# Last phase of a spectral-gate and squared-ReLU backward kernel: loads moved ahead, the gate multiply taken out of the weight-gradient copies, two terms moved to ScalarE

## The chip, the cores and the metric

The kernel runs on one core of a Trainium2 chip. The metric is the device time of one execution in microseconds: the median of nine runs before the change is 430.44 us (427.58 to 432.5). One execution was also taken by the hardware profiler; its span, from the first to the last instruction, is 428.8 us, and that execution's own time is 430.61 us.

A core has five engines that each run their own instruction list in order: TensorE (PE in the profile, its weight loads PEld) for matmuls, VectorE (DVE), ScalarE (ACT), GpSimd (POOL) and SyncE (SP), which here only issues DMAs. They wait for each other by semaphores. An engine that waits holds up all that stands behind in its own list.

## The reference, cut to what matters

The program computes a forward pass and all its gradients. `A_ref` is a 2-D real FFT of the normalized rows, multiplied by complex weights, and transformed back; `B_ref` is a two-layer MLP with squared ReLU; both stand behind a layer norm with a scale and a shift, and a gate, that come from a condition vector `c`.

```
mod = silu(c) @ w_mod                      # sa, ca, ga, sb, cb, gb
h = layernorm(x) * (1 + ca) + sa
x = x + ga * A_ref(h, A_w_r, A_w_i)        # irfft2(rfft2(h) * W)
h = layernorm(x) * (1 + cb) + sb
x = x + gb * B_ref(h, B_w1, B_b1, B_w2, B_b2)
return x
# reference(): the output, and the vector-Jacobian product with grad_out for
# A_x, A_w_r, A_w_i, B_w1, B_b1, B_w2, B_b2, c, w_mod
```

Sizes: 2048 rows of 512, a hidden size of 1792, all in bf16. The last phase of the kernel, which the change is about, produces three of the gradients. The gradient of `B_w2` is (squared ReLU of h) transposed times (gb * grad_out), 1792x512. That of `B_b2` is the column sum of gb * grad_out. That of `A_x` goes through the inverse transform of the spectral gradient and then the layer norm's backward formula, for each row: gx = v + n * a + b + gx1, where n is the normalized row, v the scaled gradient row, a and b two scalars of the row, and gx1 the gradient that came through the residual.

## The kernel before, in words

**Stages.** The forward spectral part and its back products run first (0 to about 100 us), then the MLP in four blocks of 512 rows, forward and backward (to about 283 us). Results that are needed later go to DRAM: the normalized rows (`n1_dram`), the squared ReLU (`h_dram`), the residual gradient (`gx1_dram`), the spectra. The rest is the end of the backward pass, in three stages:

1. *Spectral gradient* (`spec_f23` with `ew_b` and `after_b`, about 283 to 339 us). Eight groups `gi` of frequencies. Each group's weight gradients are made in a tile `gW` (three buffers in pool `ewb`, line 1166) and written by four DMAs (six for group 0) with rows of 257 elements (line 1170). Between the groups, `fill_w1` puts units of the `B_w1` gradient on TensorE (line 1126: 16 matmuls of 128x448 each), and `gms` emits columns of the `w_mod` gradient. `after_b` also issues the loads for what follows: the transform table `LG`, the first two tiles `hn` of the transposed squared ReLU (line 1067, DMA transposes), and all of grad_out as `g_sb` (line 1188, one DMA of 2 MB).
2. *`spec_g1`* (about 336.6 to 345.3 us). For each group TensorE makes two tiles `psG`; DVE copies one of them, ACT the other, into `CS` (lines 351 and 353).
3. *Row loop* (about 346 us to the end). Eight pairs of row tiles. For each pair: four small matmuls per tile into `psT` (line 375), a scaled copy `Tsb` on ACT (line 377), a matmul into `psY` (line 385), a copy `gs` on ACT, and then `row_pair`: on DVE the unfolding (lines 266 to 270), three products and row sums (lines 1278, 1281, 1285), the term gn = n * a + b (line 1289), and two sums (lines 1290, 1292); on ACT a scaled copy with a row sum (line 1280). The rows n1 and gx1 that it needs are loaded by `load_rows3` (lines 1222 and 1223). Between pairs, `fill` puts units on TensorE: first what is left of the `B_w1` gradient, then the 14 units `grad_w2` (line 1203: 16 matmuls of 128x512 into a PSUM buffer `mm`, of which there are two). DVE multiplies each `mm` by the gate row `modb[:, GB_B]` into `gw` (line 1206), and SyncE writes it out.

**What sets the order.** Engine lists are made by a scheduler that works through the program in the order written, by priorities (`high_priority`, `Priority`); `issue_after(x)` keeps an instruction behind x in the list. SyncE issues nearly all DMAs, in one list, on one hardware queue; eight counters are used in turn, so each DMA's issue waits until the one eight before it has landed. GpSimd issues a few writes on a queue of its own.

**Pools.** Tiles live in pools that are allocated and released like a stack at either end of the on-chip memory. When a pool is put where an earlier pool lay, the first instruction that writes a tile there waits for the last users of the old tiles in that place. In the kernel before, `gwp` (the tiles `gw`) is allocated behind `fin` (the loaded rows n1 and gxl), both after the spectral gradient, and `fin2` (the tiles `Tsb`, `gs`, `gn` and the rest of the row loop) follows at the same end when `spb` (the `Z` tiles) and `lg2` (the table `LG`) have been released.

Of the kernel before, what the change touches and what calls it, by code (L numbers as in the profile page):

```python
# [18 lines left out]
D = 512  # L19
# [316 lines left out]
def spec_g1(tc, K, Z, CS):  # L336
    nc = tc.nc
    with tc.tile_pool(name="psG", bufs=4, space=PSUM) as psG_pool, tc.tile_pool(name="psF", bufs=1, space=PSUM) as psF_pool:
        psF = psF_pool.tile([P, 4, P], FP32, name="psF")
        for gi in range(8):  # L340
            for hh in range(2):
# [8 lines left out]
                if hh == 0:  # L350
                    nc.vector.tensor_copy(out=dst, in_=src)
                else:
                    nc.scalar.copy(out=dst, in_=src)

            if gi % 2 == 1:
                for ri in range(2):
                    for n in range(2 * gi - 2, 2 * gi + 2):
                        q = 32 * (n % 4)
                        nc.tensor.matmul(psF[q:q + 1, n // 4, :], lhsT=Z[n // 2][:, n % 2, ri, 256:257], rhs=K["LG"][:, n, ri + 1, :],
                                         start=(ri == 0), stop=(ri == 1), tile_position=(0, q))  # L360
        for i in range(4):
# [82 lines left out]
class GMod:  # L444
# [13 lines left out]
    def emit(self, jc, q, row, pool, ppool):  # L458
# [8 lines left out]
        for dc in range(0, 4, 2):  # L467
            wmc = self.tiles[jc][dc // 2]
            gwm = pool.tile([P, 2, D], BF16, name="gwm", bufs=2)
# [11 lines left out]
def kernel(  # L481
# [580 lines left out]
    def load_hn():  # L1062
        fc = len(hns)
        if fc < NFC:
            pool = hnp if fc < 2 else endp.get("hn", endp["gw"])
            hns.append(pool.tile([P, NT, P], BF16, name="hn", bufs=2 if pool is not endp.get("hn") else 4))
            nc.sync.dma_start(hns[fc], h_dram[fc, :, :], transpose=True)

    lf2 = tc.alloc_tile_pool(name="lf2", bufs=1, side="right")
    gmp = tc.alloc_tile_pool(name="gmp", bufs=1, side="right")  # L1070
# [22 lines left out]
    def add_quadrants(ps, pool, out, scale=None):  # L1093
# [6 lines left out]
        def add():  # L1100
# [5 lines left out]
            if scale is not None:  # L1106
                nc.vector.tensor_tensor(row, row, scale, op=ALU.mult)
# [6 lines left out]
    def run_later(n=1):  # L1114
        if later:
            later[0][0] -= n
            if later[0][0] <= 0:
                later.pop(0)[1]()

# [29 lines left out]
    with tc.tile_pool(name="f23b", bufs=2) as fr, tc.tile_pool(name="ewb", bufs=2) as ew:  # L1149
# [22 lines left out]
        def after_b(gi):  # L1172
            if gi + 4 < 8:
                load(gi + 4)
            if gi == 3:
                with tc.issue_after(K["gW"]):
                    nc.sync.dma_start(K["LG"], LG_dram)
            fill_w1(2 if 0 < gi < 6 else 1)
            if gi == 4:
                with tc.issue_after(K["gW"]):  # L1180
                    load_hn()
                    load_hn()
            if gi == 5:
# [3 lines left out]
                with tc.issue_after(K["gW"]):  # L1187
                    K["g_load"] = nc.sync.dma_start(endp["g_sb"], g_view).ins
            if gi in (0, 1, 3, 4):
                gms.pop(0)[1]()  # L1190
                if len(gms) > 1:
                    gm.load(gms[1][0], gmp)
# [3 lines left out]
    fin = tc.alloc_tile_pool(name="fin", bufs=2, side="right")  # L1196
# [3 lines left out]
    def grad_w2(fc):  # L1200
        ps = mmps.tile([P, SB], FP32, name="mm")
# [3 lines left out]
        with tc.high_priority():  # L1205
            nc.vector.tensor_tensor(gw, ps, modb[:, GB_B, :], op=ALU.mult)  # L1206
        nc.sync.dma_start(out6_view[:, fc, :], gw)
        load_hn()

    def grad_b2():  # L1210
# [4 lines left out]
        add_quadrants(ps, gwp, out_7[None, :], modb[0:1, GB_B, :])  # L1215

    rows3 = {}

    def load_rows3(t):
        if t < NT:  # L1220
# [151 lines left out]
```

## Time and profile before

| | |
|---|---|
| median of nine runs | 430.44 us (427.58 to 432.5) |
| the profiled execution's time | 430.61 us |
| its span, first to last instruction | 428.8 us |
| busy over the span: PE / DVE / ACT / POOL | 396.3 / 354.5 / 256.2 / 55.1 us |
| clock granted to TensorE, mean | 0.994 of full |
| `spec_g1` on TensorE | 336.6 to 345.3 us |
| row loop, first `Tsb` to last `grad_w2` matmul | 348.6 to 423.6 us |

How to read it: a matmul is shown with the time from its start to its modelled end, and matmuls overlap, so that the distance between the starts of two matmuls is what one costs, and a busy PE is not yet a PE at its peak. DVE and ACT instructions overlap a little as well. Times after the first column are from the span's start. In a timeline, the bracket behind a row holds the idle time of that engine just before it and what ended the idle time. A DMA has two times: that of its issue on SyncE, and that of its landing.

### The profile page before, as it was taken

What the parts mean: (1) busy time and instruction counts of PE and PEld (TensorE: products, weight loads), DVE (VectorE), ACT (ScalarE), POOL (GpSimd) and SP (SyncE); (2) the same over time, 40 slices, a digit from 0 to 9 for tenths busy, and PEclk for the clock granted to TensorE, in tenths of its full rate; (3) what the DMA queues carried; (4) which work ended last, traced back from release to release, by engine and by line L of the source; (5) the groups of instructions that cost most, each with busy time, mean ns of one, the idle gap of its engine ahead of it and who ended that gap; (6) DMA issues with size and microseconds to landing.
All of it is one profiled execution on the core that took longest, in us unless ns stands there. A gap on an engine that the chain in (4) does not pass through costs nothing.

```text
span 428.8 us, 7116 instructions
## 1 busy us (share of the span) xinstructions
PE 396.3 (92%) x2353; PEld 195.3 (46%) x2375; DVE 354.5 (83%) x862; ACT 256.2 (60%) x487; POOL 55.1 (13%) x135
## 2 busy tenths in 40 slices
PE   2789999999899999999999999999999999897995
PEld 0344456654444444444444444455555654343332
DVE  6889868959996488968897998937997946998994
ACT  5578699678881187348635855464756464636331
POOL 7447930000000000000000000002221000000011
PEclk9999999999999999999999999999999999999899
DMA  8999899979496469778966998989999989999993
GB/s 240 222 264 299 238 241 314 294 247 203 159 357 219 122 115 336 186 159 199 299 170 179 172 311 261 298 177 313 281 275 294 175 237 189 223 276 265 261 248 116
DMA packets 144228, 101.11 MB, mean 236 GB/s; under 512 B 98970, under 2 KB 127519, under 8 KB 143807
## 3 DMA queue, kind: packets, MB, share of 16 engines
q1 hardware_dynamic: 141034, 93.03, 83.9%
q0 software_dynamic: 2592, 7.09, 5.4%
q10 hardware_dynamic: 564, 0.53, 0.4%
q8 instruction: 19, 0.31, 0.3%
q14 instruction: 19, 0.15, 0.1%
HBM read 35.44 MB, written 41.60 MB: 180 GB/s over the span
## 4 chain that ended last, share of the span: by engine, by line
PE 34%; DVE 25%; DMA 16%; ACT 14%; issue 5%; SPq 3%; POOL 2%; ACTq 0%; DVEq 0%
PE og L906 10%; PE mm L877 8%; DMA out_dram<-gW 6%; PE mm L712 5%; PE mm L1203 3%; DMA n<-n_dram 2%; DMA Xb<-xs_dram 2%; DVE jk L1285 2%; ACT gab L717 2%; PE psG L346 2%; DMA h_dram<-h 1%; DMA y<-gx_dram 1%; DMA wmc<-in_w_mod_dram 1%; ACT AE L329 1%; DMA out_dram<-x 1%
## 5 line engine op out<-in xcount | busy, mean ns | idle before, releaser
L712 PE MATMUL mm<-gT,w2T 128*128 128x512 bf16 x224 | 57.7, 383 | 3.1 <-ACT gab L717 3.1
L877 PE MATMUL mm<-h2T,w 128*128 128x512 bf16 x224 | 53.4, 378 | 1.6 <-ACT r L879 1.4
L1203 PE MATMUL mm<-g_sb,hn 128*128 128x512 bf16 x217 | 50.8, 382 | 2.3 <-DVE gw L1206 1.7
L906 PE MATMUL og<-w1T,gab 128*128 128x512 bf16 x218 | 49.9, 379 | 1.0 <-DVE o L971 0.8
L1126 PE MATMUL mm<-gab,h_sb 128*128 128x448 bf16 x256 | 50.7, 352 | 0.0
L906 PE MATMUL og<-w,h 128*128 128x512 bf16 x217 | 49.1, 379 | 0.3
L879 ACT ACTIVATE r<-mm,b1col 128x512 bf16<-128x512 f32 x56 | 37.0, 685 | 6.1 <-PE mm L877 3.3
L877 PEld LDWEIGHTS <-w 128*128 128x128 bf16 x224 | 21.1, 97 | 30.0 <-issue 8.3
L1203 PEld LDWEIGHTS <-hn 128*128 128x128 bf16 x224 | 21.4, 98 | 29.2 <-issue 5.8
L1126 PEld LDWEIGHTS <-h_sb 128*128 128x128 bf16 x256 | 24.6, 98 | 21.8 <-issue 0.6
L906 PEld LDWEIGHTS <-h 128*128 128x128 bf16 x224 | 21.8, 98 | 26.1 <-issue 0.9
L906 PEld LDWEIGHTS <-gab 128*128 128x128 bf16 x224 | 21.6, 98 | 25.9 <-issue 1.4
L712 PEld LDWEIGHTS <-w2T 128*128 128x128 bf16 x224 | 21.2, 98 | 22.6 <-issue 6.6
L1280 ACT ACTIVATE gs<-gn,inv 128x512 bf16<-128x512 bf16 x16 | 11.4, 715 | 24.8 <-DVE gn L1278 24.8
L919 ACT CAST G<-og 128x512 bf16<-128x512 f32 x16 | 9.2, 580 | 28.1 <-PE og L906 28.1
L295 POOL MEMSET AE<- 128x2 bf16 x4 | 0.3, 101 | 194.6 <-PE mm L877 194.6
L477 POOL DMA_DIRECT2D out_dram<-gwm x12 | 8.7, 730 | 118.4 <-DVE gx L1292 57.6
L881 DVE TENSOR_TENSOR h<-r 128x1024 bf16<-128x1024 bf16 x28 | 19.2, 687 | 4.8 <-ACT r L879 4.8
L717 ACT CAST gab<-mm 128x512 bf16<-128x512 f32 x36 | 21.3, 599 | 1.7 <-PE mm L712 1.5
L475 DVE SCALAR_TENSOR_TENSOR gm_junk<-wmc,onef,gmbc 128x512 bf16<-128x512 bf16 x24 | 18.0, 748 | 3.2 <-ACT gmbc L465 1.5
L715 DVE CAST gab<-mm 128x512 bf16<-128x512 f32 x20 | 13.8, 688 | 7.1 <-PE mm L712 6.8
L377 ACT ACTIVATE Tsb<-psT 128x512 bf16<-128x512 f32 x32 | 18.4, 607 | 1.5 <-PE psT L375 1.5
(290 smaller groups left out, 800.7 us busy)
## 6 DMA issues: line engine op xcount, KB each, us to landing
h_dram<-h SPq DMA_DIRECT2D x28, 256.0 KB, 3.3
gh_dram<-gab SPq DMA_DIRECT2D x28, 256.0 KB, 4.5
w<-in_B_w_dram SPq DMA_DIRECT2D x2, 1792.0 KB
wmc<-in_w_mod_dram SPq DMA_DIRECT2D x12, 256.0 KB, 5.3
out_dram<-gwm POOLq DMA_DIRECT2D x12, 256.0 KB, 6.4
wz_dram<-Z SPq DMA_DIRECT2D x8, 258.0 KB, 4.0
xs_dram<-Xs SPq DMA_DIRECT2D x8, 258.0 KB, 4.1
Z<-wz_dram SPq DMA_DIRECT2D x8, 258.0 KB, 5.7
```

What stands on the lines that cost most here:

```text
L377: nc.scalar.activation(Tsb, ps, AF.Copy, scale=EF_S)
L475: nc.vector.scalar_tensor_tensor(out=junk, in0=wmc[:, i, :], scalar=K["onef"], in1=gmbc, op0=ALU.mult, op1=ALU.mult, accum_out=self.gsc[:, ...
L712: nc.tensor.matmul(ps, lhsT=w2T[:, dc, fc * P:(fc + 1) * P], rhs=gT[b][:, :, dc, :], start=(dc == 0), stop=(dc == 3))
L715: nc.vector.tensor_copy(out=gaT[b][:, fc, :], in_=ps)
L717: nc.scalar.copy(out=gaT[b][:, fc, :], in_=ps)
L877: nc.tensor.matmul(ps, lhsT=w1[:, dc, (fc + i) * P:(fc + i + 1) * P], rhs=h2T[b][:, :, dc, :], start=(dc == 0), stop=(dc == 3))
L879: nc.scalar.activation(r[:, i, :], ps, AF.Relu, bias=b1col[:, fc + i:fc + i + 1])
L881: nc.vector.tensor_tensor(h2, r, r, op=ALU.mult)
L906: nc.tensor.matmul(ps, lhsT=lhs(fc), rhs=rhs[:, fc, :], start=(fc == 0), stop=(fc == NFC - 1))
L1126: nc.tensor.matmul(ps[:, 0:W4], lhsT=h2_sb[:, t, dc * P:(dc + 1) * P], rhs=ghn[t // 4][:, t % 4, fs], start=(t == 0), stop=(t == NT - 1))
L1203: nc.tensor.matmul(ps, lhsT=hns[fc][:, t, :], rhs=g_sb[:, t, :], start=(t == 0), stop=(t == NT - 1))
L1280: nc.scalar.activation(gs[:, i, :], gn[:, i, :], AF.Copy, scale=inv1[:, t + i:t + i + 1], accum_out=rr[:, i, 0:1])
```

## The change

- `grad_w2` no longer multiplies by the gate: its PSUM tile is copied to `gw` by ACT. Instead `g_sb` itself is multiplied by the gate row on DVE, in four pieces of 128x2048, one behind each of the last four groups of `spec_g1` (`scale_g`, called by the new argument `after`). `grad_b2`, which sums the same `g_sb`, loses its multiply at the end.
- The term gn = n * a + b of `row_pair` is made by ACT (an Identity activation with a scale and a bias per row) and no longer by DVE.
- Loads: those for the first two row pairs are issued behind `LG` in group 3 and no longer behind the last `gW` writes. `g_sb` is loaded in four DMAs of 0.5 MB behind the `gW` writes of group 4 and no longer behind those of group 5; the first two `hn` follow it and no longer go ahead of the writes of group 5. Row loads run three pairs ahead (`load_rows3(t + 6)`), the third of them in a tile of `fin2`. Each later `hn` is held behind a row load. The tiles `wmc` for the last two columns of the `w_mod` gradient are loaded together when t is 10.
- Pools: `fin` is allocated before the spectral gradient, so it no longer lies between the others; the order of releases follows. `gwm` gets four buffers at the end, and `b4` of `grad_b2` goes to another pool.

```diff
--- before.py
+++ after.py
@@ -333,7 +333,7 @@
         f3(7)
 
 
-def spec_g1(tc, K, Z, CS):
+def spec_g1(tc, K, Z, CS, after=None):
     nc = tc.nc
     with tc.tile_pool(name="psG", bufs=4, space=PSUM) as psG_pool, tc.tile_pool(name="psF", bufs=1, space=PSUM) as psF_pool:
         psF = psF_pool.tile([P, 4, P], FP32, name="psF")
@@ -348,7 +348,7 @@
                 dst = CS[:, :, :, n, :].rearrange("p t c b -> p c t b")
                 src = ps.rearrange("p h (y t b) -> p (h y) t b", y=2, b=8)
                 if hh == 0:
-                    nc.vector.tensor_copy(out=dst, in_=src)
+                    K["cast"] = nc.vector.tensor_copy(out=dst, in_=src).ins
                 else:
                     nc.scalar.copy(out=dst, in_=src)
 
@@ -358,6 +358,8 @@
                         q = 32 * (n % 4)
                         nc.tensor.matmul(psF[q:q + 1, n // 4, :], lhsT=Z[n // 2][:, n % 2, ri, 256:257], rhs=K["LG"][:, n, ri + 1, :],
                                          start=(ri == 0), stop=(ri == 1), tile_position=(0, q))
+            if after:
+                after(gi)
         for i in range(4):
             dst = CS[0:1, :, 1, i:16:4, :].rearrange("p t m b -> p m t b")
             src = psF[32 * i:32 * i + 1, :, :].rearrange("p m (t b) -> p m t b", b=8)
@@ -455,7 +457,7 @@
         for dc in range(0, 4, 2):
             self.tc.nc.sync.dma_start(self.tiles[jc][dc // 2], self.wm_view[:, dc:dc + 2, cs])
 
-    def emit(self, jc, q, row, pool, ppool):
+    def emit(self, jc, q, row, pool, ppool, nbuf=2):
 
         nc, K = self.tc.nc, self.K
         cs = slice(jc * D, (jc + 1) * D)
@@ -466,7 +468,7 @@
         junk = pool.tile([P, D], BF16, name="gm_junk", bufs=1)
         for dc in range(0, 4, 2):
             wmc = self.tiles[jc][dc // 2]
-            gwm = pool.tile([P, 2, D], BF16, name="gwm", bufs=2)
+            gwm = pool.tile([P, 2, D], BF16, name="gwm", bufs=nbuf)
             for i in range(2):
                 if i == 0:
                     nc.scalar.activation(gwm[:, i, :], gmbc, AF.Copy, scale=self.scf[:, dc + i:dc + i + 1])
@@ -1064,9 +1066,11 @@
         if fc < NFC:
             pool = hnp if fc < 2 else endp.get("hn", endp["gw"])
             hns.append(pool.tile([P, NT, P], BF16, name="hn", bufs=2 if pool is not endp.get("hn") else 4))
-            nc.sync.dma_start(hns[fc], h_dram[fc, :, :], transpose=True)
+            with tc.issue_after(K["rows" if fc < 4 else "rows0"]):
+                nc.sync.dma_start(hns[fc], h_dram[fc, :, :], transpose=True)
 
     lf2 = tc.alloc_tile_pool(name="lf2", bufs=1, side="right")
+    fin = tc.alloc_tile_pool(name="fin", bufs=2, side="right")
     gmp = tc.alloc_tile_pool(name="gmp", bufs=1, side="right")
     K["LF"] += [lf2.tile([P, 2, 3, P], BF16, name=f"LFb{gi}") for gi in range(4, 8)]
     W4 = 448
@@ -1090,7 +1094,7 @@
         nc.scalar.copy(out=b4, in_=ps[:, 0:W4])
         nc.gpsimd.dma_start(out_5.rearrange("(q f) -> q f", q=NFB), b4[0:P:32, :])
 
-    def add_quadrants(ps, pool, out, scale=None):
+    def add_quadrants(ps, pool, out):
         w = ps.shape[-1]
         b4 = pool.tile([P, w], BF16, name="b4", bufs=1)
         b4l = pool.tile([P, w], BF16, name="b4l", bufs=1)
@@ -1103,8 +1107,6 @@
                 nc.tensor.matmul(ps[0:1, 0:w], lhsT=K["ones_col"], rhs=x, start=(i == 0), stop=(i == 1))
             row = pool.tile([1, w], BF16, name="b4r", bufs=2)
             nc.scalar.copy(out=row, in_=ps[0:1, 0:w])
-            if scale is not None:
-                nc.vector.tensor_tensor(row, row, scale, op=ALU.mult)
             nc.sync.dma_start(out, row)
 
         later.append([4, add])
@@ -1116,6 +1118,16 @@
             later[0][0] -= n
             if later[0][0] <= 0:
                 later.pop(0)[1]()
+
+    rows3 = {}
+
+    def load_rows3(t):
+        if t < NT:
+            pool, n = (endp["fp"], 1) if t % 6 == 4 else (fin, 2)
+            rows3[t] = [pool.tile([P, 2, D], BF16, name=x, bufs=n) for x in ("n1", "gxl")]
+            nc.sync.dma_start(rows3[t][0], n1_dram[:, t:t + 2, :])
+            K["rows0"] = K.get("rows")
+            K["rows"] = nc.sync.dma_start(rows3[t][1], gx1_dram[:, t:t + 2, :]).ins
 
     w1o = {}
 
@@ -1175,64 +1187,63 @@
             if gi == 3:
                 with tc.issue_after(K["gW"]):
                     nc.sync.dma_start(K["LG"], LG_dram)
+                    load_rows3(0)
+                    load_rows3(2)
             fill_w1(2 if 0 < gi < 6 else 1)
+            if gi in (0, 1, 3, 4):
+                gms.pop(0)[1]()
+                if len(gms) > 1:
+                    gm.load(gms[1][0], gmp)
             if gi == 4:
-                with tc.issue_after(K["gW"]):
-                    load_hn()
-                    load_hn()
-            if gi == 5:
                 gmp.release()
                 endp["g"] = tc.alloc_tile_pool(name="gsp", bufs=1, side="right")
                 endp["g_sb"] = endp["g"].tile([P, NT, D], BF16, name="g_sb")
                 with tc.issue_after(K["gW"]):
-                    K["g_load"] = nc.sync.dma_start(endp["g_sb"], g_view).ins
-            if gi in (0, 1, 3, 4):
-                gms.pop(0)[1]()
-                if len(gms) > 1:
-                    gm.load(gms[1][0], gmp)
+                    for t in range(0, NT, 4):
+                        K["g_load"] = nc.sync.dma_start(endp["g_sb"][:, t:t + 4, :], g_view[:, t:t + 4, :]).ins
+                with tc.issue_after(K["g_load"]):
+                    load_hn()
+                    load_hn()
 
         spec_f23(tc, K, UT, AEs, None, lambda gi: gwa.tile([P, 2, 2, FP], BF16, name="G", bufs=2), ew_b, after_b)
     g_sb = endp["g_sb"]
-    fin = tc.alloc_tile_pool(name="fin", bufs=2, side="right")
     gwp = tc.alloc_tile_pool(name="gwp", bufs=1, side="right")
     endp["gw"] = gwp
 
     def grad_w2(fc):
+        if fc > 0:
+            load_hn()
         ps = mmps.tile([P, SB], FP32, name="mm")
         for t in range(NT):
             nc.tensor.matmul(ps, lhsT=hns[fc][:, t, :], rhs=g_sb[:, t, :], start=(t == 0), stop=(t == NT - 1))
         gw = gwp.tile([P, D], BF16, name="gw", bufs=3)
         with tc.high_priority():
-            nc.vector.tensor_tensor(gw, ps, modb[:, GB_B, :], op=ALU.mult)
+            nc.scalar.copy(out=gw, in_=ps)
         nc.sync.dma_start(out6_view[:, fc, :], gw)
-        load_hn()
 
     def grad_b2():
         ps = psX.tile([P, D], FP32, name="mm")
         for t in range(NT):
             q = 32 * (t % 4)
             nc.tensor.matmul(ps[q:q + 32, :], lhsT=K["ones_q"], rhs=g_sb[:, t, :], start=(t < 4), stop=(t >= 12), tile_position=(0, q))
-        add_quadrants(ps, gwp, out_7[None, :], modb[0:1, GB_B, :])
-
-    rows3 = {}
-
-    def load_rows3(t):
-        if t < NT:
-            rows3[t] = (fin.tile([P, 2, D], BF16, name="n1"), fin.tile([P, 2, D], BF16, name="gxl"))
-            nc.sync.dma_start(rows3[t][0], n1_dram[:, t:t + 2, :])
-            nc.sync.dma_start(rows3[t][1], gx1_dram[:, t:t + 2, :])
-
-    with tc.issue_after(K["g_load"]):
-        load_rows3(0)
-        load_rows3(2)
-    for _ in range(2):
-        load_hn()
+        add_quadrants(ps, endp["gm"], out_7[None, :])
 
     CS = utcs.tile([P, NT, 4, 16, 8], BF16, name="utcs")
-    spec_g1(tc, K, Z, CS)
+
+    def scale_g(gi):
+        if gi >= 4:
+            gs = g_sb[:, 4 * gi - 16:4 * gi - 12, :]
+            with tc.issue_after(K["cast"]):
+                nc.vector.tensor_tensor(gs, gs, modb[:, GB_B, None, :].broadcast_to([P, 4, D]), op=ALU.mult)
+
+    spec_g1(tc, K, Z, CS, scale_g)
     sp.release()
     lg2.release()
     fp = tc.alloc_tile_pool(name="fin2", bufs=2, side="right")
+    endp["fp"] = fp
+    load_rows3(4)
+    for _ in range(2):
+        load_hn()
     psX = tc.alloc_tile_pool(name="psX", bufs=1, space=PSUM)
     units2 = [lambda fc=fc: grad_w2(fc) for fc in range(NFC)]
 
@@ -1244,13 +1255,9 @@
                     gwa.release()
                     gap.release()
                     endp["hn"] = endp["gm"] = tc.alloc_tile_pool(name="endp", bufs=2)
-                    endp["more"] = 4
             elif units2:
                 units2.pop(0)()
                 run_later()
-                if endp.get("more", 0) > 0:
-                    endp["more"] -= 1
-                    load_hn()
 
     with tc.tile_pool(name="psE", bufs=2, space=PSUM) as psE, tc.tile_pool(name="psS1", bufs=1, space=PSUM) as psS1:
 
@@ -1286,12 +1293,12 @@
                                                accum_out=rr[:, i, 1:2])
             nc.vector.tensor_scalar(rr[:, :, 2:4], rr[:, :, 0:2], -1.0 / D, None, op0=ALU.mult)
             for i in range(2):
-                nc.vector.tensor_scalar(gn[:, i, :], n1[:, i, :], rr[:, i, 3:4], rr[:, i, 2:3], op0=ALU.mult, op1=ALU.add)
+                nc.scalar.activation(gn[:, i, :], n1[:, i, :], AF.Identity, scale=rr[:, i, 3:4], bias=rr[:, i, 2:3])
             nc.vector.tensor_tensor(gs, gn, gs, op=ALU.add)
             gx = fp.tile([P, 2, D], BF16, name="gx")
             nc.vector.tensor_tensor(gx, gs, gxl, op=ALU.add)
             nc.sync.dma_start(out1_view[:, t:t + 2, :], gx)
-            load_rows3(t + 4)
+            load_rows3(t + 6)
 
         Ts = g2_pair(0)
         for t in range(0, NT, 2):
@@ -1301,6 +1308,9 @@
             fill(1 if t % 4 == 0 and t < 12 else 0)
             if t == 10:
                 grad_b2()
+                with tc.issue_after(K["rows"]):
+                    gm.load(0, endp["gm"])
+                    gm.load(1, endp["gm"])
         fill(1)
         late.flush()
         acc1_odd = fp.tile([64, D], FP32, name="acc1_odd", bufs=1)
@@ -1309,8 +1319,7 @@
         nc.vector.tensor_tensor(acc1_sb, acc1[0:64, :], acc1_odd, op=ALU.add)
         fill(1)
         for j in range(2):
-            gm.load(j, endp["gm"])
-            gm.emit(j, 32 * j, acc1_sb[32 * j:32 * j + 1, :], endp["gm"], psX)
+            gm.emit(j, 32 * j, acc1_sb[32 * j:32 * j + 1, :], endp["gm"], psX, 4)
             fill(1)
         while units2:
             fill(1)
@@ -1327,8 +1336,8 @@
     psX.release()
     fp.release()
     gwp.release()
+    endp["g"].release()
     fin.release()
-    endp["g"].release()
     lf2.release()
     hnp.release()
     h2p.release()
```

## The prediction

> **What bounds the kernel now.** First the busy times by stretch (columns: stretch, its length, busy us and instructions of PE, PEld, DVE, ACT and POOL, granted TensorE clock, DMA share, GB/s):
>
> ```profile
> 345.00:357.00 12.00, 11.97 (x85) 6.51 (x84) 4.02 (x8) 7.77 (x17) 0.54 (x1) 1.00 0.93 239
> 357.00:390.00 33.00, 31.43 (x187) 14.08 (x187) 30.58 (x72) 15.98 (x37) 0.54 (x1) 1.00 1.04 243
> 394.00:400.00 6.00, 3.53 (x13) 0.92 (x12) 5.87 (x16) 3.18 (x8) 0.00 (x0) 0.72 0.98 241
> 400.00:424.00 24.00, 22.40 (x104) 9.11 (x104) 22.64 (x58) 9.10 (x18) 2.90 (x4) 1.00 0.87 224
> ```
>
> From 357 on DVE is busy 93 to 98% and TensorE is close behind; ACT is half idle. In 345 to 357 DVE is mostly idle. The chain of waits says what it waits for there:
>
> ```profile
> 341.06 11.63 DMA out_dram<-gW
> 352.71 4.39 DMA n<-n_dram
> 357.12 0.69 DVE q L1281
> ```
>
> The first row load stands behind the gW writes in SyncE's list, so the row loop's arithmetic starts at 357.12. TensorE does not suffer: it has units of the B_w1 gradient. What TensorE loses comes later, in its timeline:
>
> ```profile
> 366.45 3.61 PE L1203 MATMUL mm<-g_sb,hn 128*128 128x512 bf16 x15 [1.00 <-DVE gw L1206]
> ...
> 396.75 1.07 PE L385 MATMUL psY<-Tsb,TAT 128*128 128x512 bf16 x2 [2.25 <-ACT Tsb L377]
> 397.75 0.61 PE L1262 MATMUL acc<-gh,ones_q 128*32 128x512 bf16 x1
> ```
>
> Each is a wait on DVE, directly or by way of ACT. TensorE's own work sets the floor. From the starts of its matmuls: a unit of grad_w2 is 3.45 us (357.07 to 360.52), the psY, acc and psT between units 1.31 (360.52 to 361.83). From the first psY (349.29) to the last grad_w2 matmul (423.56) are 74.3 us. Of these are work: 14 x 3.45 = 48.3; 31 matmuls of B_w1, 5.9; first psY and psT 1.03, second 0.88; five times 1.31; 0.86 for the last psY pair; three more acc groups 1.0; grad_b2 0.98; small ones 1.0. Sum 66.5. So 7.8 us are lost to waits on DVE and to the slow clock after one of them, and that is all that relief of DVE can bring.
>
> **The change part by part.**
>
> *Taken off DVE:* 14 gw multiplies (684 ns, about 0.60 apart in a row), 16 gn (407 ns, 0.33 apart), one row of 0.41: 8.4 + 5.3 + 0.4 = 14.1 us of the 63.1 that it is busy from 357 to 424. A pair then costs DVE about 5.4 us for 7.1. TensorE needs 4.76 or 8.2 us per pair, so DVE is no longer the bound.
>
> *Added to ACT:* 14 copies like L717 of the same shape (585 ns) and 16 Identity activations like L940 (810 ns): 8.2 + 13.0 = 21.2 us at most, on 28.7 us that ACT is busy from 357 to 424. 50 of 67 us still fit, but ACT's list is served in order: a gw copy waits behind two gn, and a late copy holds one of two mm buffers. Followed through the new lists, no mm is missed by more than 0.2 us. I take 0.2; end of range 2.
>
> *Added to DVE in spec_g1:* four multiplies of 128x2048. The trace has none; by the 128x1024 one (688 ns, 0.61 apart) one costs 1.2 to 1.4 us, 5 in all. psG has four buffers, which covers them; CS is complete near 352 for 348.1. TensorE has two units of B_w1 there.
>
> *Moved loads:* four row loads of 256 KB go ahead of the gW writes of groups 4 to 7, the g pieces and both hn; g and hn go ahead of the writes of groups 5 to 7. No bytes are added, but what is last changes: the gW writes.
>
> *The new wait.* fin used to lie between other pools and no longer does. So fin2 now begins where the gW tiles lay; before, the gw tiles lay there. In the built program's order with its waits, the first Tsb on ACT, and the first unfolding on DVE, wait on all eight counters of SyncE's queue, at counts that belong to the eight gW writes of groups 6 and 7. Before, that Tsb waited on loads of Z, Xb and LG, long landed; it ran at 348.64. Behind it on ACT stand all gs, gn and gw copies; TensorE waits at psY, SyncE's third row load waits for the same landings.
>
> When do these writes land? Before, SyncE's hn behind them goes at 356.67:
>
> ```profile
> 341.06 9.40 SPq L1170 DMA_DIRECT2D out_dram<-gW  x8
> 352.71 0.33 SPq L1222 DMA_DIRECT2D n<-n_dram  x1
> 353.09 0.63 SPq L1223 DMA_DIRECT2D gxl<-gx_dram  x1
> 353.76 0.73 SPq L1222 DMA_DIRECT2D n<-n_dram  x1
> 354.94 0.32 SPq L1223 DMA_DIRECT2D gxl<-gx_dram  x1
> 356.67 2.19 SPq L1067 DMA_TRANSPOSE hn<-h_dram  x1
> ```
>
> Two ways. (1) DMA was busy 93 to 108% in these stretches. What goes ahead of the last write grows by the four row loads; two such landed at 357.10 and 358.39 with one between, 0.65 each: 356.6 + 2.6 = 359.2. (2) By the issue order: the g pieces land near 344 (2 MB took 5.9 us behind the writes before it), two hn after that at 2.6 each, the second issued by 347.2. From the end of the second hn's issue the writes of group 5 landed 6.1 to 6.6 us later; the writes of group 7 wait, one for one, for those of group 5 (eight counters), are 0.6 apart and need at least 4.6: 347.2 + 6.6 + 0.6 + 4.6 = 359.0, and up to 1.8 more if they queue. I take 360; 357.4 if the loads fill gaps in the queue, 364 if the hn stretch as at 326.87, where two took SyncE 10.85 us.
>
> TensorE comes to psY at 349.29 + 3.2 (17 more B_w1 matmuls stand ahead of it now) = 352.5 and goes on at 360 + 0.65 = 360.65 (before, Tsb started at 348.64 and psY at 349.29). It idles 8.2 us, which nothing covers.
>
> *Clock.* The stretch 394 to 400 shows clock 0.72 after the idle 2.25 us: 2.37 us went (396.75 to 399.12) where 1.08 of work and 0.22 of wait are due, so 1.1 lost. [...] By the row the sum below is 0.4 lower[...]; I take 1.5[...].
>
> *Other losses after the start:* the fifth hn is issued behind the second pair's output, about 17.3 us after Tsb, and lands 4.6 to 6.6 later where its unit begins at 22.8: 0.5. The tail behind the last matmul (423.56 to 428.8) stays: an ACT copy of 0.59 for a DVE one of 0.68.
>
> *Sum.* After psY 66.5 - 3.2 = 63.3 of work, and 0.2 + 1.5 + 0.5 = 2.2 lost. 360.65 + 63.3 + 2.2 = 426.15, where before it was 423.56: +2.6. Against the profiled execution, 430.61 + 2.6 = 433.2; that execution lies 0.17 above the median of 430.44, so 433.0.
>
> **The rivals.**
>
> *Slower by the late start (0.52):* as summed, 433.0; own range 431.8 to 436.
>
> *Still slower (0.16):* the writes land at 364, since the two hn and the GpSimd writes beside them stretch the queue, and the hn of units 5 and 6 are 2 us late: +4 + 2, 439. For it: hn issues of 7.2 us in this trace. Against it: most took 2.2 to 4.4.
>
> *It cancels (0.18):* the writes land near 357.4. Then the idle 5.6 and losses of 2.2 equal the 7.8 won: 430.4. For it: DMA is only 69% busy in 340 to 344, and that gap could be filled by g, which is ready earlier.
>
> *Faster (0.14):* the wait is there but does not bite, because the gW writes land before TensorE comes to psY. Alone among writes they landed in 4.6 to 6.5 us after issue. Landing by 352.0, nothing idles, the clock holds, and 7.8 - 0.7 = 7.1 come out: 423.3. Below a landing of 357.4 it decides for faster. Against it: the 11.63 us of the chain, behind one g load, and now both hn lie ahead too.
>
> That a part does nothing is no rival: the work on DVE does go.
>
> **How the numbers follow.** The measurement of this kernel can tell about 0.3%, 1.3 us, from no change. Slower by more: 0.52 + 0.16 = 0.68. Within: 0.18. Faster: 0.14. The predicted time is the likeliest case's, 433.0. The range leaves out half of the faster case and part of the worst: 428.5 to 438. Slower cases hold most of the chance; the likeliest one's own range is 431.8 to 436.
>
> **What would show it.** In the profile after: the first Tsb of the row loop on ACT with idle time ended by a gW write, starting near 360; psY on TensorE behind 7 to 9 us idle, with a granted clock below 0.8 there; then the row loop's DVE busy under 85%, gaps of TensorE on DVE nearly gone, from that psY to the last grad_w2 matmul about 65.5 us for 74.3. Wrong would be: a first Tsb before 357; a row loop still over 70 us, with TensorE waiting on ACT's gw copies or for hn; or a TensorE that waits in spec_g1 for the scaled g.

## The result, and the profile after

The changed kernel takes 438.0 us (median of ten runs, 434.25 to 441.37) where the kernel before took 430.49 (32 runs, 427.58 to 432.89): a ratio of 1.0165, with a 95% interval of 1.0139 to 1.0191. It is slower, as forecast, but by 7.5 us and not by 2.6. The ratio leaves out the execution of 441.37 us, which lies 1.6% above the fastest of the ten; by the ratio the loss is 7.1 us. The profiled execution took 438.42 us with a span of 436.6 us, 7.8 more than before.

First the busy times of the changed kernel by the same stretches as those shown of before, with the same columns:

```profile
345.00:357.00 12.00, 8.05 (x57) 4.17 (x54) 5.65 (x7) 2.71 (x5) 0.54 (x1) 1.00 0.60 130
357.00:390.00 33.00, 27.96 (x155) 13.58 (x159) 24.17 (x57) 26.13 (x54) 0.54 (x1) 0.90 0.67 163
394.00:400.00 6.00, 5.95 (x50) 2.72 (x50) 4.71 (x9) 4.01 (x10) 0.00 (x0) 1.00 0.94 227
400.00:424.00 24.00, 19.50 (x97) 7.82 (x97) 17.61 (x43) 16.60 (x33) 1.20 (x2) 1.00 1.04 242
```

VectorE is no longer full: 24.17 of 33 us for 30.58, and 17.61 of 24 for 22.64. ScalarE has taken the work. Yet TensorE does less than before in three of the four stretches. The timelines say where. ScalarE first (start, duration, line and operation, and in brackets the idle time just before and what ended it):

```profile
351.38 0.58 ACT L369 CAST utcs<-psF 1x512 bf16<-1x512 f32 x1 [0.75 <-DVE utcs L367]
359.79 1.08 ACT L379 ACTIVATE Tsb<-psT 128x512 bf16<-128x512 f32 x2 [7.83 <-DMA out_dram<-gW]
```

The first Tsb of the row loop waits 7.83 us for a gW write and starts at 359.79, where the prediction put the landing at 360. TensorE in the same view:

```profile
352.45 0.73 PE L1138 MATMUL mm<-gab,h_sb 128*128 128x448 bf16 x3
360.44 0.59 PE L387 MATMUL psY<-Tsb,TAT 128*128 128x512 bf16 x1 [7.25 <-ACT Tsb L379]
...
373.53 0.38 PE L387 MATMUL psY<-Tsb,TAT 128*128 128x512 bf16 x1 [0.33 <-ACT Tsb L379]
...
386.34 6.85 PE L1218 MATMUL mm<-g_sb,hn 128*128 128x512 bf16 x31 [1.17 <-DMA hn<-h_dram]
...
402.75 3.63 PE L1218 MATMUL mm<-g_sb,hn 128*128 128x512 bf16 x16 [2.39 <-DMA hn<-h_dram]
...
413.13 1.68 PE L1218 MATMUL mm<-g_sb,hn 128*128 128x512 bf16 x7 [1.90 <-DMA hn<-h_dram]
```

There are two kinds of loss. One is at the start: 7.25 us of idleness at psY, and then a slow clock. The next row has the same columns as the first ones above; the third number from the end is the granted clock, 0.69 of full:

```profile
360.44:366.77 6.33, 6.33 (x34) 3.45 (x34) 2.82 (x6) 3.51 (x8) 0.00 (x0) 0.69 0.90 196
```

In these 6.33 us TensorE did about 4.56 us of work (the same instructions at the distances that they have in the kernel before at full clock), so 1.8 were lost. The other was hardly forecast: TensorE waits three times for a tile hn, for the fifth, the eighth and the tenth (units of grad_w2 counted from the first at 366.77), 5.5 us in all. None of its waits is for VectorE any more. SyncE's list of DMA issues shows why hn comes late (start and time of the issue):

```profile
346.51 8.57 SPq L1182 DMA_DIRECT2D out_dram<-gW  x12
359.66 0.35 SPq L1128 DMA_DIRECT2D n<-n_dram  x1
...
394.64 0.49 SPq L1130 DMA_DIRECT2D gxl<-gx_dram  x1
395.17 7.05 SPq L1070 DMA_TRANSPOSE hn<-h_dram  x2
...
404.36 2.06 SPq L458 DMA_DIRECT2D wmc<-in_w_mod_dram  x4
406.51 4.55 SPq L1070 DMA_TRANSPOSE hn<-h_dram  x1
```

SyncE is issuing nearly throughout from 380.6 to 413.8: some 31 of 33.2 us, of which the seven hn issues take 22.9. The hn whose landing ends the 2.39 us is issued at 395.17, right behind the row load that the change holds it behind, and the last one shown stands behind four wmc loads. The chain of waits, which runs through the same places, agrees:

```profile
388.05 4.49 SPq L1070
...
395.17 7.54 DMA hn<-h_dram
402.75 3.63 PE mm L1218 x16
406.38 0.14 PE psY L387
406.51 6.58 DMA hn<-h_dram
```

By the prediction's own marks: the first psY at 360.44 (360.65 was forecast), from there to the end of the last grad_w2 matmul 71.9 us (65.5), and behind it 4.2 us (5.2 before). A row loop of over 70 us with waits for hn is one of the signs of being wrong that the prediction named.

### The profile page after: what moved, and what is told of

Same layout as the page of the kernel before. It is cut to its first block, busy times and chain, and to the rows that moved or that the text cites. A ratio compares the mean times of both kernels' runs of the same rounds, so it can differ in the third digit from the quotient of the medians.

```text
span 436.6 us, 7131 instructions
## 1 busy us (share of the span) xinstructions
PE 397.5 (91%) x2353; PEld 196.5 (45%) x2375; DVE 346.1 (79%) x835; ACT 275.0 (63%) x517; POOL 54.6 (13%) x135
## 5 line engine op out<-in xcount | busy, mean ns | idle before, releaser
L1218 PE MATMUL mm<-g_sb,hn 128*128 128x512 bf16 x217 | 49.7, 379 | 5.9 <-DMA hn<-h_dram 5.5
L1138 PE MATMUL mm<-gab,h_sb 128*128 128x448 bf16 x256 | 51.9, 358 | 0.0
L1142 ACT CAST gw<-mm 128x448 bf16<-128x448 f32 x16 | 8.6, 540 | 22.5 <-PE mm L1138 22.5
```

The lines of the kernel that those rows point to most:

```text
L1138: nc.tensor.matmul(ps[:, 0:W4], lhsT=h2_sb[:, t, dc * P:(dc + 1) * P], rhs=ghn[t // 4][:, t % 4, fs], start=(t == 0), stop=(t == NT - 1))
L1218: nc.tensor.matmul(ps, lhsT=hns[fc][:, t, :], rhs=g_sb[:, t, :], start=(t == 0), stop=(t == NT - 1))
```

## The experiments

The kernel before took 427.5 to 431.4 us in the different sets of runs, so each run is told as a ratio to the kernel before in its own set, with a 95% interval; 0.1% is 0.43 us. A letter, as in "theory A", means the theory of that letter in the expectation printed just above the result; the same letter means different things in different runs.

### The place of fin2

In the memory layout of the two built programs, fin2 ended 192 bytes below the pool `ewb` of the gW tiles before (96,704 to 129,920; ewb begins at 130,112). After, gwp begins 4 KB higher, because the tiles b4 of grad_b2 left it, and fin2, which ends where gwp begins, now ends at 134,016, 3.9 KB inside ewb. (Its own new pair n1 and gxl makes it 4 KB larger too, but at the other end, which changes nothing here.) Its first users wait for all last users of ewb, the gW writes among them. The wait is between the pools as wholes: the first Tsb lies at 100,800, far below ewb, and the gW tiles lie from 138,432 on, above the end of fin2.

Two runs test this, one from each side. The first puts fin2 below ewb again in the changed kernel (acc1_odd moves too, which makes fin2 2 KB smaller):

```diff
-        add_quadrants(ps, endp["gm"], out_7[None, :])
+        add_quadrants(ps, gwp, out_7[None, :])
...
-        acc1_odd = fp.tile([64, D], FP32, name="acc1_odd", bufs=1)
+        acc1_odd = endp["gm"].tile([64, D], FP32, name="acc1_odd", bufs=1)
```

> The changed kernel with the small tiles of grad_b2 back in gwp and acc1_odd in endp, so that fin2 ends below the place of the gW tiles; all loads and all engine moves stay. Theory A (the new wait comes from fin2 reaching 3.9 KB into the place of the gW tiles): the first Tsb no longer waits for a gW write, psY comes when TensorE is there, near 353 for 360.4; the idle 7.25 us and about 1.8 us of slow clock after it go, the three waits for hn (6.0 us) stay or move: 438.0 - 9.0 = 429, 428 to 431. Theory B (the start is late because the queue's loads are late, whatever the place): first Tsb or the first product with n1 still near 359, 437 to 438.5.

Measured: 0.9993 (0.9975 to 1.0012), 427.26 us where the kernel before took 427.54. Theory A. The first Tsb on ScalarE now waits only for TensorE (in the built program, for loads that landed long before):

```profile
353.67 1.09 ACT L379 ACTIVATE Tsb<-psT 128x512 bf16<-128x512 f32 x2 [0.52 <-PE psT L377]
```

and the list of TensorE's waits from 345 on (us in total, times, longest) keeps the hn:

```profile
PE mm L1218 <- DMA hn<-h_dram: 3.9, 2, 2.1
PE psY L387 <- ACT Tsb L379: 0.7, 1, 0.7
```

The second makes the overlap in the kernel before, and changes nothing else:

```diff
-        add_quadrants(ps, gwp, out_7[None, :], modb[0:1, GB_B, :])
+        add_quadrants(ps, endp["gm"], out_7[None, :], modb[0:1, GB_B, :])
```

> The kernel BEFORE with one edit: the small tiles of grad_b2 go to endp, so that gwp is 4 KB smaller and fin2 reaches into the place of the gW tiles; loads and engines as before. Theory A (place alone makes the wait): the first Tsb waits for gW writes, near 356.7 for 348.64, and TensorE idles about 7 us at psY. The kernel before has 7.8 us of waits on DVE later in which part of this disappears, and DVE did about 3.5 us of work before 357: 434, 432 to 438. Theory B (the loads moved ahead make the wait): no such wait, 430.5.

Measured: 1.0194 (1.0145 to 1.0242) from four executions, some 8 us slower: theory A. ScalarE in its timeline:

```profile
355.50 1.08 ACT L377 ACTIVATE Tsb<-psT 128x512 bf16<-128x512 f32 x2 [7.52 <-DMA gxl<-gx_dram]
```

The trace names a row load, which comes back on the same eight counters; in the built program this Tsb waits for the gW writes of groups 6 and 7, as in the changed kernel. Moving 4 KB of small tiles is enough for the wait, without any change to loads or engines. The price was above the 4 us expected: I had set part of it off against the waits on VectorE that this kernel has anyway.

### The hn loads

The next run keeps the wait and gives the hn loads back the places they had in the kernel before:

```diff
-            with tc.issue_after(K["rows" if fc < 4 else "rows0"]):
-                nc.sync.dma_start(hns[fc], h_dram[fc, :, :], transpose=True)
+            nc.sync.dma_start(hns[fc], h_dram[fc, :, :], transpose=True)
...
     def grad_w2(fc):
-        if fc > 0:
-            load_hn()
...
         nc.sync.dma_start(out6_view[:, fc, :], gw)
+        load_hn()
...
                     endp["hn"] = endp["gm"] = tc.alloc_tile_pool(name="endp", bufs=2)
+                    endp["more"] = 4
...
                 run_later()
+                if endp.get("more", 0) > 0:
+                    endp["more"] -= 1
+                    load_hn()
```

> The changed kernel with the hn loads issued as in the kernel before: no wait behind a row load in SyncE's list, called at the end of each grad_w2, and four extra ones once endp exists. Theory A (hn is late because of its place in SyncE's list): the three waits of TensorE for hn (1.17, 2.39 and 1.90 us in the profile) go, 438.0 - 6.0 = 432, 431 to 434; the late start at 360.4 stays. Theory B (the queue is full, so that what is loaded earlier only delays something else): TensorE waits instead for rows by way of DVE, or for hn all the same, 436.5 to 438.5.

Measured: 1.0072 (1.0038 to 1.0106) for the changed kernel's 1.0165: about 4 us back, from six executions. In its profile no matmul waits for hn any more (the weight loads do once, for 0.4 us). Its idle time at the first psY is 4.56 us there, for 7.25: the landing of the gW writes moves by some 3 us from one profile to the other (psY at 357.06 there, for 360.44), and a part of the 4 us may be that.

Both repairs together:

> Both edits together: fin2 off the place of the gW tiles, and the hn loads as in the kernel before. If the two losses are separate and add up: 438.0 - 9.0 - 6.0 = 423, faster than the kernel before by 7.5 us, which is the time that its TensorE lost to DVE. If the earlier start runs into the loads, since the third and fourth hn still wait for the gW writes to land near 359 and the clock of the queue is what counts: 427 to 430.

Measured: 1.0095 (1.0057 to 1.0134) from four executions. Neither expectation was right: the second repair makes the first one worse. Since it rested on four executions, it was run again:

> The kernel with both repairs (fin2 off the place of the gW tiles, hn loads as in the kernel before, gn on ScalarE) once more, with more executions, since 1.0095 rested on four. If the repairs do not add up: 1.006 to 1.013. If that was chance: 0.996 to 1.003, as the profile of that run (span 427.4 us) would have it.

Measured: 1.0071 (1.0046 to 1.0096). The repairs do not add up, and this profile shows why. SyncE's list, then VectorE's timeline, then TensorE's:

```profile
365.02 9.54 SPq L1069 DMA_TRANSPOSE hn<-h_dram  x3
...
375.72 3.38 SPq L1069 DMA_TRANSPOSE hn<-h_dram  x1
379.20 0.53 SPq L1302 DMA_DIRECT2D out_dram<-gx  x1
```

```profile
363.85 0.68 DVE L1301 TENSOR_TENSOR gx<-gs,gxl 128x1024 bf16<-128x1024 bf16 x1
...
369.12 0.68 DVE L1301 TENSOR_TENSOR gx<-gs,gxl 128x1024 bf16<-128x1024 bf16 x1
...
382.88 0.69 DVE L1301 TENSOR_TENSOR gx<-gs,gxl 128x1024 bf16<-128x1024 bf16 x1 [7.75 <-issue]
```

```profile
385.28 0.38 PE L387 MATMUL psY<-Tsb,TAT 128*128 128x512 bf16 x1 [1.81 <-ACT Tsb L379]
388.04 0.59 PE L387 MATMUL psY<-Tsb,TAT 128*128 128x512 bf16 x1 [2.38 <-ACT Tsb L379]
```

Four hn issues occupy SyncE nearly all the time from 365.0 to 379.1, and the first gx, made at 363.85, is written out only behind them, from 379.20. There are two gx tiles. VectorE stands still for 7.75 us before it makes the third gx, which starts 3.7 us after the issue of that first write; "issue" means that the trace names no releaser, so that it is the tile it waits for is my reading. TensorE then waits 4.2 us for Tsb, and its granted clock falls (0.81 on average from 390 to 400). If the hn go last, TensorE waits for them; if they go first, VectorE does not get rid of its output.

How much the late hn cost was then measured by leaving them out:

```diff
-        if fc < NFC:
+        if 4 <= fc < NFC:
+            hns.append(hns[fc % 4])
+        elif fc < NFC:
             pool = hnp if fc < 2 else endp.get("hn", endp["gw"])
```

In the changed kernel with fin2 below ewb:

> The changed kernel with fin2 off the place of the gW tiles, and with the hn loads from the fifth on left out: units 4 to 13 of grad_w2 multiply the first four tiles again, so the gradient of B_w2 is wrong in those columns; all matmuls, copies and writes stay. It says what the relief of VectorE is worth when no hn load stands in the way. Theory A (the relief is real, 7.8 us, and the late hn loads ate it): TensorE's 3.9 us of waits for hn go, rows and outputs come sooner too: ratio to the kernel before 0.983 to 0.988, 421.5 to 424. Theory C (the turns between VectorE and ScalarE in the row chain take the place of the waits at once): 0.993 to 0.999.

In the kernel before:

> The same in the kernel BEFORE: hn loads from the fifth on left out, units 4 to 13 multiply the first four tiles again (the gradient of B_w2 is wrong there). In its profile TensorE never waits for hn. Theory A (VectorE bounds its row loop): nothing gained, ratio 0.997 to 1.002. Theory E (the DMA queue bounds it by way of the rows n1 and of the gw buffers, though no wait of TensorE names it): 0.985 to 0.993.

Measured: 0.986 (0.9814 to 0.9906, from four executions) and 0.9996 (0.9973 to 1.0018). Theory A in both. Without hn loads in the way the changed kernel is 1.4% faster than before, and the list of TensorE's waits has nothing left but

```profile
PE psY L387 <- ACT Tsb L379: 2.2, 2, 1.5
PE acc L1271 <- DVE gh L270: 0.3, 1, 0.3
```

The kernel before gains nothing: its TensorE waits for VectorE as it did, at the largest

```profile
368.62 3.61 PE L1205 MATMUL mm<-g_sb,hn 128*128 128x512 bf16 x16 [1.46 <-DVE gw L1208]
...
398.27 0.86 PE L385 MATMUL psY<-Tsb,TAT 128*128 128x512 bf16 x2 [1.64 <-ACT Tsb L377]
```

So VectorE did bound the kernel before, and what lies between the two is what the relief is worth together with the moved loads: 1.4%, 5.9 us (about 2 either way by the two intervals).

### gn on ScalarE

The kernel before, with the last of the changes to engines alone:

```diff
-                nc.vector.tensor_scalar(gn[:, i, :], n1[:, i, :], rr[:, i, 3:4], rr[:, i, 2:3], op0=ALU.mult, op1=ALU.add)
+                nc.scalar.activation(gn[:, i, :], n1[:, i, :], AF.Identity, scale=rr[:, i, 3:4], bias=rr[:, i, 2:3])
```

> The kernel BEFORE with one part of the change: gn = n * a + b made by ScalarE (two Identity activations a pair) and not by VectorE. Theory A (VectorE's load is what TensorE waits for in the kernel before, and relief pays one for one up to the 7.8 us lost): 5.3 us off VectorE, of which the start until 357 is not touched: 427.5 - 3.5 = 424, 423 to 426. Theory C (the row chain is a chain of turns between VectorE and ScalarE, and each activation of 0.81 us put in it costs more than the 0.41 us it takes off, the more so behind other ScalarE work): 427.5 to 430.

Measured: 1.000 (0.9971 to 1.003). Theory C: 5.3 us off the engine that bounds the loop brought nothing. In its profile VectorE now waits 3.7 us in four places for gn, and TensorE waits 2.5 us for VectorE's gh and 1.7 for Tsb. The reverse edit was made in four of the kernels above and below:

> The changed kernel with fin2 off the place of the gW tiles, and with gn back on VectorE; hn loads as the change has them. TensorE lost 3.9 us to hn and 0.7 to ScalarE there. Theory A (VectorE's relief carries the gain): slower by 1 to 4 us than with gn on ScalarE (ratio to the kernel before 0.9993), 428.5 to 431.5. Theory C (gn on ScalarE is worth nothing or less, since TensorE waits for hn): same within 1 us, 426 to 428, or faster where an earlier gx lets SyncE issue the hn behind it earlier.

> The kernel with both repairs (fin2 off the place of the gW tiles, hn loads as before), and with gn back on VectorE. There TensorE waited 4.1 us for Tsb on ScalarE, once with both gn activations (1.52 us) between two Tsb. Theory C (gn on ScalarE makes these waits): they go, the ratio to the kernel before falls from 1.0095 to 1.000 or below, 425 to 427.5. Theory A (VectorE's relief is worth its time there): slower still by up to 3 us, 431 to 434. Theory D (the order of the hn loads itself costs what e3 lost to e1): no change, 430 to 431.5.

> The changed kernel with fin2 off the place of the gW tiles, without the hn loads from the fifth on (the gradient of B_w2 is wrong in those columns), and with gn back on VectorE. With gn on ScalarE the ratio to the kernel before was 0.986. Theory A (each us off VectorE pays): 5.3 us back on it, 0.992 to 0.998. Theory C (the relief comes from the gw multiplies, gn on ScalarE pays nothing): 0.983 to 0.989.

> The version with hn one row earlier (fin2 off the place of the gW tiles, wmc early, hn held one pair earlier; 0.994), with gn back on VectorE. Theory A: 0.998 to 1.004. Theory C: 0.990 to 0.995.

| kernel | gn on ScalarE | gn on VectorE |
|---|---|---|
| before | 1.000 (0.9971 to 1.003) | 1 |
| fin2 below ewb | 0.9993 (0.9975 to 1.0012) | 1.0046 (1.0023 to 1.007) |
| fin2 below ewb, no later hn | 0.986 (0.9814 to 0.9906) | 0.9885 (0.9844 to 0.9926) |
| fin2 below ewb, wmc early, hn one row earlier | 0.994 (0.9917 to 0.9964) | 0.9966 (0.994 to 0.9992) |
| fin2 below ewb, hn as before | 1.0071 (1.0046 to 1.0096) | 0.9993 (0.9971 to 1.0016) |

In the second row gn on ScalarE pays 0.5%, about 2 us; in the third and fourth the difference of 0.25% lies within the intervals. Against 5.3 us taken off VectorE that is little. Most of the 5.9 us therefore seems to come from the rest of the change, the gw multiplies or the moved loads; no run separates these two. In the last row it costs 0.8%. There VectorE waits 2.7 us before a gx when gn is on VectorE, for 7.75. That fits the reading above; whether gn itself or the order of hn and gx in SyncE's list makes the difference was not tried.

### Where the loads should stand

Two small moves of loads, with fin2 below ewb. First the wmc loads without their hold, which puts them ahead of the row loop:

```diff
-                with tc.issue_after(K["rows"]):
-                    gm.load(0, endp["gm"])
-                    gm.load(1, endp["gm"])
...
+            gm.load(j, endp["gm"])
             gm.emit(j, 32 * j, acc1_sb[32 * j:32 * j + 1, :], endp["gm"], psX, 4)
```

> The changed kernel with fin2 off the place of the gW tiles, and the four wmc loads (1 MB) issued where the program writes them without a hold, which puts them behind the fourth hn and ahead of the row loads, near 362, and no longer between the ninth and tenth hn. The tenth hn, late by 1.79 us in the profile of the kernel without this edit, should be in time, the seventh (2.11 us) not: 427.3 - 1.8 = 425.5, 424.5 to 427. If the 1 MB in front delays the first rows or hn instead: 427.3 to 430.

Measured: 0.9977 (0.9955 to 0.9999). The wait for the tenth hn is gone, so wmc made that one late; but the fifth is now late by 1.38 us and the eighth (called the seventh in the text above) by 2.27. In time it can't be told from the kernel without the edit (0.9993). On top of it, two ways to have hn earlier. Each held behind a row load one pair earlier:

```diff
-            with tc.issue_after(K["rows" if fc < 4 else "rows0"]):
+            with tc.issue_after(K["rows"] if fc < 4 else K["rows00"]):
...
+            K["rows00"] = K.get("rows0")
             K["rows0"] = K.get("rows")
```

> The changed kernel with fin2 off the place of the gW tiles, wmc early, and each hn from the fifth on held behind a row load one pair earlier (K rows00 for rows0). Without that hold moved: ratio 0.9977, with 1.38 and 2.27 us of waits for hn and 1.5 us of slow clock after the second. Theory A: these go, 0.988 to 0.993. If the loads only change places in a full queue (theory D): 0.996 to 1.002.

or one more hn loaded ahead, once:

```diff
                     endp["hn"] = endp["gm"] = tc.alloc_tile_pool(name="endp", bufs=2)
+                    endp["more"] = 1
...
                 run_later()
+                if endp.get("more", 0) > 0:
+                    endp["more"] -= 1
+                    load_hn()
```

> As the run before, but in place of the moved hold one hn more is loaded ahead, once, when endp exists, so that all later hn are one unit ahead of their use; the hold stays as the change has it. Theory A: the waits for hn go, 0.988 to 0.993. Theory D (full queue): 0.996 to 1.002.

Measured: 0.994 (0.9917 to 0.9964) and 0.9953 (0.9928 to 0.9977), both faster than the kernel before and the changed kernel, and both between the two expectations. In the profile of the first of these TensorE has the same waits in the row loop, of 2.2 and 0.3 us, as in the kernel without later hn, and none for hn; in that of the second one wait for hn of 2.4 us is left. Why the first is still 0.8% behind the kernel without later hn stays open. A part may lie ahead of the row loop, where TensorE waits 1.2 us in spec_g1 in that profile. In the profile of the second, VectorE waits in group 7 for a gW tile whose earlier content has not yet been written out:

```profile
341.63 0.43 DVE L422 TENSOR_TENSOR gW<-p 128x514 bf16<-128x514 bf16 x1 [2.33 <-DMA out_dram<-gW]
```

and TensorE waits 2.73 us in spec_g1 behind it. The moved loads stand ahead of those writes in all of these kernels; in the profile of the changed kernel this wait does not occur.

## Why the prediction was right or wrong

The ratios make a chain of four steps from the kernel before to the changed one, in microseconds of 430: leave out the later hn, 0.2 less; relieve VectorE and move the loads, 5.9 less; load the hn again as the change has them, 5.7 more; let fin2 reach into ewb, 7.4 more. The sum is 7.0, which is the measured result by the way the chain is built (7.1 by the ratio, but for rounding). The 5.9 and the 5.7 are known to about 2 us, the 7.4 to about 1.4. Against it stand the prediction's 7.6 (7.8 less the 0.2 taken for ScalarE), 0.5 and 9.7 (8.2 of idleness and 1.5 of clock).

**The relief of VectorE: right in place, a little high.** No wait of TensorE for VectorE is left in the row loop; 7.6 us were forecast and 5.9 measured (with the moved loads), within an interval that holds the forecast. The prediction counted the 16 gn like the 14 gw multiplies; alone, in the kernel before, the gn paid nothing (1.000, 0.3% either way).

**The new wait: right, with a wrong reason.** Place, engine and time were right: ScalarE's Tsb at 359.79 for 360, 7.25 us of idleness for 8.2. That the time came so near is in part luck: in the profile of the kernel with the hn as before, psY came at 357.06. And I said that fin2 begins where the gW tiles lay because fin no longer lies between. The runs show that 4 KB of gwp decide: the wait comes in the kernel before, with fin where that kernel has it, and goes in the changed kernel, with fin where the change puts it. In the medians it costs 7.4, less than the profile's idle time and slow clock together (9.0).

**The clock: sized well, in part by luck.** 1.8 us were lost, for 1.5. In the trace of the changed kernel the granted clock is 0.50 from 357.58 to 364.41 and 1.00 from there to 366.77. That is the 0.69 over 6.33 us: TensorE worked 3.97 us of them at 0.50, which loses 2.0 as an estimate. The 1.1 that I read from the trace of before was too low, since I counted to 399.12 only, and the clock is 0.50 there from 396.57 to 399.98. Up to 402.67, the end of the unit that starts at 399.12, 5.92 us went where 4.53 are due (0.86 for psY and acc, 3.45 for the unit, 0.22 of wait), so 1.4 were lost. That I took 1.5 and not 1.1 was my estimate; I had not shown it from the trace. When a pause brings the slow clock is not settled here: in the kernel before 2.25 us did (0.72 from 394 to 400), and in the changed kernel 2.39 us did not (1.00 from 400 to 424).

**"Other losses after the start: the fifth hn ... 0.5": this step failed.** The fifth hn was late by 1.17 us, the eighth by 2.39 and the tenth by 1.90: 5.5 us, and 5.7 in the medians. I asked of each hn only behind which row it is held, and stopped at the first that came late; the later ones were put at nothing. Even that one was issued 20.8 us after Tsb, for 17.3. I did not follow SyncE's list as a whole. A late hn makes the row loads behind it late, behind which the next hn is held, and in the chain of waits SyncE issues with no pause above 0.06 us from 386.4 to the hn of 395.17. A full list alone does not do it: in the kernel before SyncE issues for some 30 of the 33.6 us from 380.2 to 413.8, and no hn is late. There the hn run further ahead of their units; this is its eighth, and the start of its fifth unit:

```profile
376.20 2.40 SPq L1067 DMA_TRANSPOSE hn<-h_dram  x1
376.23 3.62 PE L1203 MATMUL mm<-g_sb,hn 128*128 128x512 bf16 x15
```

In the changed kernel the eighth goes at 395.17, when the seventh unit starts (395.42). Of three units of lead the change left one, and the prediction gave that no cost; with the hn issued as before, no matmul waited for them. The four wmc loads, listed among the changes, were not costed at all; they made the tenth late.

**The scaled g: right.** The multiplies took 1.22 us each (1.2 to 1.4 forecast), and in the changed kernel's profile nothing in spec_g1 waits for them.

**The rivals.** "Faster", 423.3 us if the wait does not bite, is refuted by the run without the wait, 0.9993: the hn loads would still have taken the gain. "Still slower", 439, had the right size and named late hn, but as 2 us on two units behind a landing at 364; the first Tsb started at 359.79, and the hn are late on their own. "It cancels" needed a landing near 357.4, and no late hn.

## What to carry to other kernels

When work is taken off the engine that bounds a loop, add up next what each queue has to issue in one turn of that loop, long issues with their measured time; here SyncE was as full as the engines in both kernels (some 30 of 33.6 us before, 31 of 33.2 after), and its order decided whether TensorE waited for inputs or VectorE for its outputs. How many units ahead of its use each load is issued is a number to write down before and after. A tile moved from one pool to another is also a change of addresses: look where the pools behind it come to lie, since 4 KB cost 7 to 8 us here, though neither the tile that waited nor the gW tiles lie where the two pools overlap, and nothing in the diff's arithmetic or loads shows it. And test a repair together with the others: two that each brought 4 us or more brought about 4 together.

## What the runs showed of the hardware that was not expected

A transposing load occupied SyncE for 2.0 to 4.6 us in the changed kernel's row loop, where a plain row load or write mostly took 0.3 to 0.6. What makes one of them longer is open: one of 4.55 us stood right behind four plain loads of 256 KB, and one of 4.49 us right behind a row load. Nothing behind it in the list is issued in that time: the next issue came at 411.17 behind the one of 4.55 us (from 406.51) and at 392.63 behind the one of 4.49 (from 388.05).

Moving 0.81 us activations between two engines in a loop of short turns paid from 0 to 0.5%, and cost 0.8% in one kernel, where the count of busy microseconds said 1.2% (5.3 of 430). In the kernel before VectorE then waited 3.7 us for gn; that such turns between VectorE and ScalarE took the rest is argued from that profile, not shown by a run.
